# Attention, soft mixture of experts and a gated block in one kernel: one VectorE pass per weight tile instead of two, and a new order of the side work

## The chip, the cores and the metric

One core of a Trainium2 chip runs the whole program. The metric is the device time of one execution in microseconds (us); lower is better. The core has five engines that run their own instruction streams in order and wait for one another through semaphores: TensorE (PE, matrix products; PEld is its loading of weights), VectorE (DVE), ScalarE (ACT), GpSimd (POOL) and SyncE (SP, which here issues every DMA).

## The reference

Three stages follow one another, each in float32:

```python
# attention: q, k, v are (4, 8, 1152, 64); two neighbouring queries are averaged, which leaves 576
scores = scale * matmul(q_pool, k.T);  scores -= max(scores, -1)
attn = exp(scores); attn /= sum(attn, -1) + 1e-9;  x = attn @ v        # x as (2304, 512)
# soft mixture of experts: phi (512, 32), 8 experts with w1 (512, 1024) and w2 (1024, 512)
logits = x @ phi;  d = softmax over rows;  c = softmax over columns
slot_out[e] = relu((d.T @ x)[e] @ w1[e]) @ w2[e];  x = c @ slot_out
# gated block: w_gate, w_val (512, 1536), w_out (1536, 512)
xn = x / sqrt(mean(x*x) + 1e-6) * rms_g;  out = (silu(xn @ w_gate) * (xn @ w_val)) @ w_out
```

The weights of the gated block arrive as float64 words in memory and are turned into float32 on the chip; this is the conversion that the change touches.

## The kernel before

**Attention** works on 16 pairs of heads (`p` = 0 to 15). A pair has 9 key tiles of 128 keys (`kt`) and two halves of 288 queries (`h`). For each key tile and half, `qk` (L360) forms the scores in four products (L369: high and low parts of q and k, and one that subtracts the row's maximum), ScalarE takes the exponential into a tile `e` (L371), and `add_e` (L376) has GpSimd add `e` to a running sum `acc` (L385). `av` (L387) multiplies `e` with v (L391). It is not called for each key tile but after every third one, for three tiles together: these runs of 24 matrix instructions are called *visits* here, and the three key tiles ahead of a visit a *stage*. A pair is thus stage A, visit 1, stage B, visit 2, stage C, visit 3.

The maxima of pair `p+1` are made during pair `p`: 14 items, each a product into PSUM (L318, the last two L325) and a maximum over it by VectorE (L320, L326). `MAX` says how many of the first 12 follow each key tile: before, 2, 2, 1 in stage A, 2, 2, 1 in stage B and 2, 0, 0 in stage C. The last two are `max_tail`.

Scores, maxima and all small products of the side work share one ring of three PSUM buffers of two banks each (tag `u`): the product that takes a buffer waits until the engine that read the one three places earlier is done. The visits write to two other banks (tag `av`).

**Side work** of other pairs is put between the steps of a key tile by the table `AT`: the number ahead of the point is the key tile, the fraction the place within it. Before, a key tile has seven steps (`q0 m q1 m e0 e1 a`, `q` the scores of a half, `m` a maximum, `e` the addition, `a` the visit if one is due), so nothing can be placed inside a visit. For the pair behind (`l = p-1`): `take_x` copies the result out, `sums` and `recips` form the denominators (L410, L419), `x_turn` and `x_divide` transpose and scale (L434, L443), `x_logits`, `x_share` and `logit_add` make the logits (L450, L459, L469 and L470). For the pairs ahead: `load_q`, `load_k`, `load_v` issue DMAs, `sum_q` adds query pairs on GpSimd (L283), `high_q`, `round_k`, `block_q` round on ScalarE (L288, L279, L294), `low_q` and `low_k` take the rest on VectorE (L298, L304), `max_red`, `max_row` and `send_row` bring the maxima into rows (L331, L336, L338, L344). In every fourth pair (`p` = 5, 9, 13) `d_turn`, `d_exp`, `d_back`, `slot_part` and `slot_turn` serve the softmax over rows, and in the pair after it `c_soft` that over columns.

**The conversion.** 36 tiles of 128 x 512 words are loaded (`load_64`), and each takes two instructions on ScalarE (`abs_64`, L658 and L660) and two on VectorE (`turn_64`): L662 shifts the word and fills in the low bits, L663 then brings in the sign. Tiles that are done and aren't kept go back to memory (`spill`, L600), and return in the last stage. `load` (L616) fetches expert weights into whatever buffers are free; buffers come from pools with the tags W, A, B and C, and `KEEP` says how many B buffers the prefetch leaves alone.

Pairs 0 and 15 run half by half (`HALVED`, `STEP_0`), with tables of their own (`AT_0`, `AT_15`).

**After attention** the experts' weights stream through products with 32 columns, and then the gated block runs, bound by its matrix products. The change leaves both as they are, but for the buffers that the prefetch of weights may use.

Of the kernel before, what the change touches and what calls it, by code (L numbers as in the profile page):

```python
# [14 lines left out]
ALU = mybir.AluOpType  # L15
# [15 lines left out]
STEP = "q0 m q1 m e0 e1 a".split()  # L31
STEP_0 = "q m m e a".split()
VISIT = 3
MAX = [2, 2, 1, 2, 2, 1, 2, 0, 0]
AT = dict(
    low_k=[2.8, 2.96],
    low_q=5.84,
    load_v=7.3,
    max_tail=5.79,
    max_red=7.5,  # L40
    max_row=8.78,
    send_row=8.79,
    load_q=4.3,
    load_k=5.73,
    sum_q=6.05,
    high_q=6.8,
    block_q=7.0,
    round_k=[7.8, 8.3],
    take_x=0.5,
    sums=2.79,  # L50
    recips=2.95,
    x_turn=[5.8, 8.8],
    x_divide=[5.81, 8.81],
    x_logits=5.82,
    x_share=5.95,
    logit_add=6.0,
    drop_x=8.82,
    d_turn=0.5,
    d_exp=1.5,
    d_back=2.8,  # L60
    d_copy=2.95,
    slot_part=5.785,
    slot_copy=5.95,
    slot_turn=8.8,
    c_soft=[2.83, 4.5, 5.85],
    load_64=[0.86, 1.65, 4.0],
    abs_64=[2.82, 5.83, 7.4],
    turn_64=[6.2, 6.7, 7.2, 7.7, 8.2, 8.6],
# [14 lines left out]
    send_row=8.79,  # L83
    sum_q=5.91,
# [10 lines left out]
    logit_add=5.22,  # L95
    take_x_a=5.49,
# [23 lines left out]
N_B = 18  # L120
N_C = 42
# [3 lines left out]
KEEP = [7, 6, 12, 6]  # L125
# [14 lines left out]
def attention_softmoe_gated_kernel(ctx: ExitStack, tc: tile.TileContext, kT, qT, vv, ip, cst, w1, w2, wg, wv, wo, rg, out):  # L140
# [235 lines left out]
    def add_e(p, kt, h):  # L376
        e = ets[p, kt, h]
        if kt == 0:
            first[p, h] = e
            return  # L380
        if kt == 1:
            acc[p, h] = B([128, 2, HQ], F32, "acc")
        a = first[p, h] if kt == 1 else acc[p, h]
        eng = dv if p in HALVED and kt % 2 == 0 else gp
        eng.tensor_tensor(out=acc[p, h], in0=a, in1=e, op=ALU.add)  # L385
# [17 lines left out]
    def sums(p, hs=(0, 1)):  # L403

        n = len(hs)
        o = bank([64 * n, HQ], "sums")
        for s in (1, 0):
            for i, h in reversed(list(enumerate(hs))):
                g = 32 * (n * s + i)
                pe.matmul(o[g:g + 32, :], lhsT=ones, rhs=acc[p, h][:, s], start=True, stop=True)  # L410
        rel("B", n)
        srow[p] = B([64 * n, HQ], F32, "srow")
        ac.copy(srow[p], o)
# [235 lines left out]
    def abs_64(n):  # L649

        spill()
        for _ in range(min(n, len(fresh))):
# [5 lines left out]
            ac.activation(w32[key][0], hi.bitcast(F32), AF.Abs, scale=2.0 ** -112)  # L658
            top = raw.bitcast(U16).rearrange("p (n t) -> p n t", t=4)[:, :, 1]
            ac.activation(lo.bitcast(I32), top, AF.Copy, scale=2.0 ** -13, bias=-4095.5 / 8192)  # L660
            turning.extend([
                lambda y=y, lo=lo: dv.scalar_tensor_tensor(out=y, in0=y, scalar=3, in1=lo, op0=ALU.logical_shift_left, op1=ALU.bitwise_or),  # L662
                lambda y=y, hi=hi, key=key: (dv.scalar_tensor_tensor(  # L663
                    out=y, in0=hi, scalar=0x80000000, in1=y, op0=ALU.bitwise_and, op1=ALU.bitwise_or), rel("A"),
                    done.append(key) if key in out_of_chip else None),
            ])
# [7 lines left out]
    def side(p):  # L674
# [11 lines left out]
        if n < NP:  # L686
            at("low_k", lambda i: low_k(n, slice(576 * i, 576 * i + 576)))
            at("low_q", lambda i: low_q(n))
            at("load_v", lambda i: load_v(n))
            if p:  # L690
                at("max_tail", lambda i: (max_item(n, 12), max_item(n, 13)))
            at("max_red", lambda i: max_red(n))
            at("max_row", lambda i: max_row(n))
            at("send_row", lambda i: send_row(n))
# [7 lines left out]
        if l >= 0:  # L702
# [8 lines left out]
            at("logit_add", lambda i: logit_add(l))  # L711
# [15 lines left out]
        if p < NP - 1:  # L727
            at("abs_64", lambda i: abs_64(1))
            at("turn_64", lambda i: turn_64(1))
# [19 lines left out]
    with tc.manual_schedule():  # L749
# [61 lines left out]
        for p in range(NP):  # L811
# [3 lines left out]
            for u, (kt, h) in enumerate(steps):  # L815
# [3 lines left out]
                for i, step in enumerate(order):  # L819
# [11 lines left out]
                    elif kt % VISIT == VISIT - 1:  # L831
                        for k in range(kt - VISIT + 1, kt + 1):
# [415 lines left out]
```

## Time and profile before

| | |
|---|---|
| median of 3 runs | 841.74 us (840.76 to 842.36) |
| the profiled execution | 840.79 us, of which the span from first to last instruction is 839.0 us |
| busy PE / DVE / POOL / ACT | 754.5 / 536.6 / 501.8 / 444.5 us |
| mean granted TensorE clock | 0.963 |
| pairs 1 to 14 of attention | 49.62 to 548.09 us of the span |

Matrix products are pipelined and their ends are modelled, so the busy time of PE is no measure of how full it is; the idle times just before an instruction and what ended them are the better guide. In views of stretches, the columns are the stretch, its length, busy us of each engine with the number of instructions in brackets, the granted clock, the mean busy share of the 16 DMA engines, and GB/s. In lists by line a row gives line, engine, operation, output from inputs, count, then busy us and the mean ns of one, and the idle time ahead of them with what ended it.

### The profile page before, as it was taken

Reading aid. Unit: us, or ns where it says so; the run is one execution under the profiler, and the core shown is the slowest. Engines: PE = TensorE matmul, PEld = TensorE weight load, DVE = VectorE, ACT = ScalarE, POOL = GpSimd, SP = SyncE. Lnnn points to the kernel's source line nnn. Section 1 sums busy time; section 2 is a strip of 40 time slices with the busy share of each in tenths; the row PEclk is TensorE's granted clock in tenths of the full one; section 3 lists DMA queues with packets and bytes.
Section 4 is the critical chain, followed back from the end, with each engine's and each line's share of the span. In section 5 each row is a group of like instructions: output and inputs, shape, how many; then the busy total and the mean of one; then the engine's idle time right before and its main releaser. Section 6 shows DMA issues by size and latency. Waiting matters only on the chain.

```text
span 839.0 us, 15594 instructions
## 1 busy us (share of the span) xinstructions
PE 754.5 (90%) x6015; PEld 516.3 (62%) x6015; DVE 536.6 (64%) x715; ACT 444.5 (53%) x995; POOL 501.8 (60%) x372
## 2 busy tenths in 40 slices
PE   5998989988798897889989798997998999999998
PEld 3555656555465565556556555654444788888887
DVE  6858897796788877688598758724304466545430
ACT  2447566565556656565565546454323686545430
POOL 5448878785777867758697666752200675444330
PEclk9999999998999989999899998999899999999999
DMA  4231531706164351533515313243799210000001
GB/s 153 86 133 42 186 132 67 247 31 220 34 217 144 118 211 52 186 100 125 207 42 186 127 72 126 80 151 127 263 365 385 92 39 24 28 26 16 36 25 38
DMA packets 53001, 103.57 MB, mean 123 GB/s; under 512 B 5832, under 2 KB 19648, under 8 KB 52928
## 3 DMA queue, kind: packets, MB, share of 16 engines
q1 hardware_dynamic: 52928, 102.59, 34.7%
q8 instruction: 47, 0.77, 0.4%
q14 instruction: 26, 0.21, 0.1%
HBM read 89.39 MB, written 13.11 MB: 122 GB/s over the span
## 4 chain that ended last, share of the span: by engine, by line
PE 69%; DVE 14%; ACT 8%; issue 4%; DMA 4%; POOL 0%; SPq 0%; ACTq 0%; DVEq 0%; POOLq 0%
PE yo L1151 18%; PE av L391 16%; PE sc L369 15%; ACT e L371 5%; DVE mx L320 5%; PE mxp L318 4%; DMA w<-in_w_dram 3%; PE gv L1103 3%; DVE w L662 3%; PE xl L450 2%; DVE mx L326 2%; DVE w L663 1%; PE sums L410 1%; PE mxp L325 1%; PE pp L528 1%
## 5 line engine op out<-in xcount | busy, mean ns | idle before, releaser
L385 POOL TENSOR_TENSOR acc<-acc,e 128x576 f32<-128x576 f32 x208 | 329.0, 1613 | 89.9 <-ACT e L371 80.0
L371 ACT ACTIVATE e<-sc 128x576 f32<-128x576 f32 x288 | 184.1, 651 | 216.8 <-PE sc L369 211.8
L320 DVE TENSOR_REDUCE mx<-mxp 128x2 f32<-128x768 f32 x192 | 182.3, 956 | 54.5 <-PE mxp L318 47.9
L391 PE MATMUL av<-e,vt 128*64 128x288 f32 x1152 | 163.5, 434 | 0.3 <-ACT e L371 0.3
L369 PE MATMUL sc<-qh,kh 64*128 64x288 f32 x576 | 109.6, 376 | 22.9 <-DVE mx L320 16.2
L391 PEld LDWEIGHTS av<-e,vt 128*64 128x64 f32 x1152 | 82.4, 145 | 65.9 <-issue 21.5
L369 PEld LDWEIGHTS sc<-qh,kh 64*128 64x128 f32 x576 | 55.5, 188 | 82.3 <-DVE mx L320 53.7
L1151 PE MATMUL yo<-woh,hA 128*128 128x512 f32 (+1 forms) x312 | 98.9, 384 | 0.0
L385 POOL TENSOR_TENSOR acc<-e 128x576 f32<-128x576 f32 x32 | 44.9, 1416 | 80.6 <-ACT e L371 80.5
L369 PE MATMUL sc<-mr,pick 64*128 64x288 f32 x576 | 87.7, 297 | 1.0 <-DMA mr<-mrow 1.0
L369 PE MATMUL sc<-ql,kh 64*128 64x288 f32 x576 | 87.1, 297 | 0.0
L369 PE MATMUL sc<-qh,kl 64*128 64x288 f32 x576 | 87.0, 297 | 0.0
L318 PE MATMUL mxp<-kh,qh 64*128 64x384 f32 x384 | 75.6, 391 | 11.3 <-ACT kh L774 5.7
L1108 DVE SCALAR_TENSOR_TENSOR th<-th,gv 128x384 f32<-128x384 f32 x72 | 39.9, 554 | 62.6 <-ACT th L1105 62.1
L1134 POOL TENSOR_TENSOR hA<-hu,hA 128x384 fp32r<-128x384 f32 x48 | 48.9, 1018 | 42.8 <-ACT hA L1133 38.4
L662 DVE SCALAR_TENSOR_TENSOR w<-w,raw 128x512 uint32<-128x512 uint32 x36 | 64.6, 1795 | 0.0
L1151 PEld LDWEIGHTS yo<-woh,hA 128*128 128x128 f32 x312 | 57.6, 188 | 10.2 <-issue 0.7
L1105 ACT ACTIVATE th<-gv 128x384 f32<-128x384 f32 x72 | 35.3, 490 | 42.7 <-PE gv L1103 40.2
L1151 PE MATMUL yo<-wol,hA 128*128 128x512 f32 (+1 forms) x151 | 57.8, 383 | 0.0
L369 PEld LDWEIGHTS sc<-mr,pick 64*128 64x128 f32 x576 | 56.5, 190 | 1.6 <-DMA mr<-mrow 1.4
L369 PEld LDWEIGHTS sc<-qh,kl 64*128 64x128 f32 x576 | 56.6, 191 | 0.0
L369 PEld LDWEIGHTS sc<-ql,kh 64*128 64x128 f32 x576 | 56.2, 190 | 0.0
(178 smaller groups left out, 1118.1 us busy)
## 6 DMA issues: line engine op xcount, KB each, us to landing
w<-in_w_dram SPq DMA_DIRECT2D x88, 256.0 KB
w<-in_w_dram SPq DMA_DIRECT2D x20, 512.0 KB
vt<-in_vv_dram SPq DMA_DIRECT2D x16, 576.0 KB
qraw<-in_qT_dram SPq DMA_DIRECT2D x15, 576.0 KB
kraw<-in_kT_dram SPq DMA_DIRECT2D x15, 576.0 KB
away<-w SPq DMA_DIRECT2D x32, 256.0 KB
w<-away SPq DMA_DIRECT2D x32, 256.0 KB
raw<-in_wg_dram SPq DMA_DIRECT2D x12, 512.0 KB
```

The lines of the kernel that those rows point to most:

```text
L318: pe.matmul(o[:, s, 0:KC], lhsT=qh[p][r, 128 * t:128 * t + 128], rhs=kh[p][r, KC * c:KC * c + KC], start=True, stop=True)
L320: dv.reduce_max(out=to, in_=o[:, :, 0:KC], axis=AX.X)
L369: pe.matmul(o[:, s, 0:HQ], lhsT=w[r, wk], rhs=q[r, c], start=(i == 0), stop=(i == 3))
L371: ac.activation(ets[p, kt, h], o[:, :, 0:HQ], AF.Exp, scale=0.0625)
L385: eng.tensor_tensor(out=acc[p, h], in0=a, in1=e, op=ALU.add)
L391: pe.matmul(avt[p, h][64 * s:64 * s + 64, 0:HQ], lhsT=vt[p][:, kt, 64 * s:64 * s + 64], rhs=ets[p, kt, h][:, s], start=(kt == 0), stop=(kt ...
L662: lambda y=y, lo=lo: dv.scalar_tensor_tensor(out=y, in0=y, scalar=3, in1=lo, op0=ALU.logical_shift_left, op1=ALU.bitwise_or),
L1103: pe.matmul(o[i], lhsT=sg[n][:, 256 * i + 128 * c:256 * i + 128 * c + 128], rhs=cT[g], start=True, stop=True)
L1105: ac.activation(t, o[0], AF.Tanh, scale=0.5)
L1108: dv.scalar_tensor_tensor(out=t, in0=t, scalar=1.0, in1=o[0], op0=ALU.add, op1=ALU.mult)
L1134: gp.tensor_tensor(out=b, in0=u, in1=f(a), op=ALU.subtract)
L1151: pe.matmul(o, lhsT=x, rhs=w[:, c], start=(ft == 0 and i == 0), stop=(ft == NF - 1 and i == 2))
```

## The change

One VectorE pass per converted tile goes: ScalarE's first instruction becomes `Prelu` with a slope of -2^32 for negative numbers in place of `Abs`, which sets the bit that the shift then moves into the place of the sign. `spill` is called from places of its own. The running sum of `e` becomes two: one over key tiles 0 to 4, one over 5 to 8, and `sums` adds both in PSUM. All 12 maxima come in the first six key tiles. A step `b` is added: `a` now does two key tiles of a visit and `b` the third, so that side work can be placed between them; most places in `AT` are new. B buffers go from 18 to 20, C buffers from 42 to 40, and `KEEP` changes.

```diff
-STEP = "q0 m q1 m e0 e1 a".split()
-STEP_0 = "q m m e a".split()
+STEP = "q0 m q1 m e0 e1 a b".split()
+STEP_0 = "q m m e a b".split()
 VISIT = 3
-MAX = [2, 2, 1, 2, 2, 1, 2, 0, 0]
+PART = 5
+MAX = [2, 2, 2, 2, 2, 2, 0, 0, 0]
 AT = dict(
-    low_k=[2.8, 2.96],
-    low_q=5.84,
+    load_q=0.3,
+    load_k=0.31,
+    sum_q=1.5,
+    high_q=4.6,
+    round_k=[3.6, 5.3],
+    block_q=6.6,
+    low_k=[6.1, 6.3],
+    low_q=6.0,
     load_v=7.3,
-    max_tail=5.79,
-    max_red=7.5,
-    max_row=8.78,
-    send_row=8.79,
-    load_q=4.3,
-    load_k=5.73,
-    sum_q=6.05,
-    high_q=6.8,
-    block_q=7.0,
-    round_k=[7.8, 8.3],
+    max_tail=[2.87, 2.88],
+    max_red=5.9,
+    max_row=7.0,
+    send_row=7.3,
     take_x=0.5,
-    sums=2.79,
-    recips=2.95,
-    x_turn=[5.8, 8.8],
-    x_divide=[5.81, 8.81],
-    x_logits=5.82,
-    x_share=5.95,
-    logit_add=6.0,
-    drop_x=8.82,
-    d_turn=0.5,
-    d_exp=1.5,
-    d_back=2.8,
-    d_copy=2.95,
-    slot_part=5.785,
+    sums=1.9,
+    recips=2.86,
+    x_turn=[5.87, 8.85],
+    x_divide=[5.88, 8.86],
+    x_logits=8.87,
+    drop_x=8.88,
+    x_share=8.95,
+    logit_add=0.3,
+    d_turn=1.91,
+    d_exp=2.1,
+    d_back=2.85,
+    d_copy=2.855,
+    slot_part=5.86,
     slot_copy=5.95,
-    slot_turn=8.8,
-    c_soft=[2.83, 4.5, 5.85],
-    load_64=[0.86, 1.65, 4.0],
-    abs_64=[2.82, 5.83, 7.4],
-    turn_64=[6.2, 6.7, 7.2, 7.7, 8.2, 8.6],
+    slot_turn=8.86,
+    c_soft=[6.35, 7.4, 8.4],
+    load_64=[0.2, 3.0, 8.3],
+    spill=[1.4, 4.4],
+    abs_64=[2.72, 2.73, 5.73],
+    turn_64=[5.72, 7.2, 8.1],
...
-N_B = 18
-N_C = 42
+N_B = 20
+N_C = 40
...
-KEEP = [7, 6, 12, 6]
+KEEP = [10, 6, 12, 12]
...
     def add_e(p, kt, h):
-        e = ets[p, kt, h]
-        if kt == 0:
-            first[p, h] = e
+
+        j = int(kt >= PART)
+        n, e = kt - PART * j, ets[p, kt, h]
+        if n == 0:
+            first[p, h, j] = e
             return
-        if kt == 1:
-            acc[p, h] = B([128, 2, HQ], F32, "acc")
-        a = first[p, h] if kt == 1 else acc[p, h]
+        if n == 1:
+            acc[p, h, j] = B([128, 2, HQ], F32, "acc")
         eng = dv if p in HALVED and kt % 2 == 0 else gp
-        eng.tensor_tensor(out=acc[p, h], in0=a, in1=e, op=ALU.add)
+        eng.tensor_tensor(out=acc[p, h, j], in0=first[p, h, j] if n == 1 else acc[p, h, j], in1=e, op=ALU.add)
...
-        for s in (1, 0):
-            for i, h in reversed(list(enumerate(hs))):
-                g = 32 * (n * s + i)
-                pe.matmul(o[g:g + 32, :], lhsT=ones, rhs=acc[p, h][:, s], start=True, stop=True)
-        rel("B", n)
+        for j in range(2):
+            for s in (1, 0):
+                for i, h in reversed(list(enumerate(hs))):
+                    g = 32 * (n * s + i)
+                    pe.matmul(o[g:g + 32, :], lhsT=ones, rhs=acc[p, h, j][:, s], start=(j == 0), stop=(j == 1))
+        rel("B", 2 * n)
...
-            ac.activation(w32[key][0], hi.bitcast(F32), AF.Abs, scale=2.0 ** -112)
+            ac.activation(w32[key][0], hi.bitcast(F32), AF.Prelu, scale=2.0 ** -112, alpha=-2.0 ** 32)
...
-            turning.extend([
-                lambda y=y, lo=lo: dv.scalar_tensor_tensor(out=y, in0=y, scalar=3, in1=lo, op0=ALU.logical_shift_left, op1=ALU.bitwise_or),
-                lambda y=y, hi=hi, key=key: (dv.scalar_tensor_tensor(
-                    out=y, in0=hi, scalar=0x80000000, in1=y, op0=ALU.bitwise_and, op1=ALU.bitwise_or), rel("A"),
-                    done.append(key) if key in out_of_chip else None),
-            ])
+            turning.append(lambda y=y, lo=lo, key=key: (
+                dv.scalar_tensor_tensor(out=y, in0=y, scalar=3, in1=lo, op0=ALU.logical_shift_left, op1=ALU.bitwise_or),
+                rel("A"), done.append(key) if key in out_of_chip else None))
...
-                at("max_tail", lambda i: (max_item(n, 12), max_item(n, 13)))
+                at("max_tail", lambda i: max_item(n, 12 + i))
...
-            at("logit_add", lambda i: logit_add(l))
+            if p == NP - 1:
+                at("logit_last", lambda i: logit_add(l - 1))
+                at("logit_add", lambda i: logit_add(l))
+            elif l > 0:
+                at("logit_add", lambda i: logit_add(l - 1))
...
                     elif kt % VISIT == VISIT - 1:
-                        for k in range(kt - VISIT + 1, kt + 1):
+                        for k in (kt - 2, kt - 1) if step == "a" else (kt,):
```

## Rows read from the trace of the kernel before

**Rows 1.** The chain that ended last: shares of the span, by engine and by line.
```profile
PE 69%; DVE 14%; ACT 8%; issue 4%; DMA 4%; POOL 0%; SPq 0%; ACTq 0%; DVEq 0%; POOLq 0%
PE yo L1151 18%; PE av L391 16%; PE sc L369 15%; ACT e L371 5%; DVE mx L320 5%; PE mxp L318 4%; DMA w<-in_w_dram 3%; PE gv L1103 3%; DVE w L662 3%; PE xl L450 2%; DVE mx L326 2%; DVE w L663 1%; PE sums L410 1%; PE mxp L325 1%; PE pp L528 1%
```

**Rows 2.** Stretches of pair 8: A, visit 1, B, C, and the pair's sum.
```profile
299.18:305.55 6.37, 6.17 (x66) 4.24 (x67) 5.17 (x6) 4.30 (x8) 2.84 (x3) 1.00 0.91 302
305.55:308.68 3.13, 3.13 (x29) 1.70 (x26) 0.57 (x1) 1.75 (x4) 3.13 (x2) 1.00 1.05 418
308.68:317.76 9.08, 8.49 (x81) 6.22 (x80) 7.88 (x11) 5.30 (x13) 7.07 (x7) 1.00 0.17 69
...
320.89:328.90 8.01, 5.07 (x56) 3.98 (x56) 7.45 (x8) 6.18 (x12) 6.55 (x5) 1.00 0.09 33
...
sum 32.85, PE 29.11 PEld 19.55 DVE 25.14 ACT 19.99 POOL 25.86; mean PE 4.85 PEld 3.26 DVE 4.19 ACT 3.33 POOL 4.31
```

**Rows 3.** The same view of pair 14: stage C and the pair's sum.
```profile
539.86:544.96 5.10, 4.97 (x57) 3.98 (x57) 2.63 (x5) 3.56 (x7) 3.48 (x3) 1.00 0.21 80
sum 29.93, PE 29.02 PEld 19.54 DVE 20.71 ACT 15.35 POOL 21.56; mean PE 4.84 PEld 3.26 DVE 3.45 ACT 2.56 POOL 3.59
```

**Rows 4.** Waits in stage C of pair 8: total us, times, longest us.
```profile
PEld mxt L336 <- ACT kh L279: 1.8, 1, 1.8
PEld sc L369 <- DVE mx L320: 1.7, 2, 1.5
...
PE sc L369 <- DVE mx L320: 1.2, 1, 1.2
```

**Rows 5.** VectorE in pair 8 in order of time: start us, us.
```profile
300.12 5.04 DVE L320 TENSOR_REDUCE mx<-mxp 128x2 f32<-128x768 f32 x5 [2.29 <-PE mxp L318]
...
322.70 1.78 DVE L662 SCALAR_TENSOR_TENSOR w<-w,raw 128x512 uint32<-128x512 uint32 x1
```

**Rows 6.** Lines over the whole span.
```profile
L385 POOL TENSOR_TENSOR acc<-acc,e 128x576 f32<-128x576 f32 x208 | 329.0, 1613 | 89.9 <-ACT e L371 80.0 <-DVE acc L385 9.9
L371 ACT ACTIVATE e<-sc 128x576 f32<-128x576 f32 x288 | 184.1, 651 | 216.8 <-PE sc L369 211.8 <-POOL acc L385 1.1 <-PE mxp L318 0.7
...
L663 DVE SCALAR_TENSOR_TENSOR w<-raw,w 128x512 uint32<-128x512 uint32 x36 | 54.3, 1507 | 0.3
...
L470 DVE TENSOR_TENSOR lg<-lg,ls 96x192 f32<-96x192 f32 (+1 forms) x13 | 12.0, 925 | 0.4
...
L469 DVE TENSOR_TENSOR lg<-lg,ls 96x192 f32<-96x192 f32 (+1 forms) x13 | 9.8, 754 | 0.4
```

**Rows 7.** Line L470 alone: shortest, median and longest in ns.
```profile
L470 DVE TENSOR_TENSOR lg<-lg,ls x13: 253/1440/1447, 105.3 to 583.9; 96x192 f32<-96x192 f32 x11, 96x96 f32<-96x96 f32 x2
```

**Rows 8.** Small products of pair 8 on TensorE: start us, us.
```profile
308.61 0.53 PE L419 MATMUL sumt<-cs,srow 128*96 128x128 f32 x3
...
314.93 0.79 PE L325 MATMUL mxp<-kh,tb 128*128 128x384 f32 x3
...
315.81 0.53 PE L434 MATMUL xo<-cs,xu 128*96 128x128 f32 x3
...
316.59 1.23 PE L450 MATMUL xl<-ipt,xu 128*96 128x64 f32 x12 [0.26 <-DVE mx L326]
```

**Rows 9.** Stretches: pairs 1 to 4, 6 to 8, 10 to 12, summed.
```profile
sum 343.57, PE 303.95 PEld 201.54 DVE 278.97 ACT 206.97 POOL 266.96; mean PE 101.32 PEld 67.18 DVE 92.99 ACT 68.99 POOL 88.99
```

**Rows 10.** Stretches: pair 9, and pairs 5, 9 and 13 summed.
```profile
332.03:372.46 40.43, 34.20 (x304) 22.08 (x303) 28.84 (x34) 22.53 (x51) 27.32 (x18) 0.96 0.37 129
...
sum 124.97, PE 106.59 PEld 69.33 DVE 85.58 ACT 67.64 POOL 80.90; mean PE 35.53 PEld 23.11 DVE 28.53 ACT 22.55 POOL 26.97
```

**Rows 11.** Stretches: visit 3 of pair 7, and most of the experts' part.
```profile
293.64:299.18 5.54, 5.54 (x27) 2.64 (x26) 4.16 (x3) 1.32 (x6) 3.64 (x3) 0.56 0.32 105
...
599.50:650.00 50.50, 47.47 (x517) 21.62 (x516) 11.63 (x31) 14.53 (x35) 3.52 (x9) 1.00 1.03 373
```

**Rows 12.** The DMA queue's own waits over the span: total us, times, longest.
```profile
SPq L600 <- DVE w L663: 210.5, 14, 22.1
```

**Rows 13.** ScalarE's load of a function table, the only one in the span.
```profile
L768 ACT ACT_TABLE_LOAD x1 | 1.3, 1283 | 0.7 <-PEq L1237 0.7
```

More of the change, by code (lines that the diff above doesn't have):

```diff
@@ L83 @@
     send_row=8.79,
+    load_q=4.3,
+    load_k=5.73,
     sum_q=5.91,
@@ L95 @@
     logit_add=5.22,
+    logit_last=0.3,
     take_x_a=5.49,
@@ L649, in abs_64 @@
     def abs_64(n):
-        spill()
         for _ in range(min(n, len(fresh))):
@@ L727, in side @@
         if p < NP - 1:
+            at("spill", lambda i: spill())
             at("abs_64", lambda i: abs_64(1))
```

## The prediction, as it was recorded before the change was run

> **What bounds the kernel now.** I read the chain that ended last first. TensorE is 69% of it, but VectorE 14%, and within that the two conversion passes have 3% and 1% [rows 1]: some 34 us of the span end on a conversion, which is no part of attention at all. Next I cut a pair without disturbance, pair 8, into its stages and visits. All three visits take 3.13 us (one is shown) and the stages 6.37, 9.08 and 8.01 [rows 2]. In stage C, TensorE has 5.07 us of work in 8.01. Its waits name the reasons: two score products stood behind maxima, 1.7 and 1.2 us, and the transposition of the maxima waited 1.8 us for ScalarE's rounding of k [rows 4]. VectorE's order in time says why the maxima were late: a conversion pass of 1.78 us starts at 322.70, amid the maxima of key tile 6 [rows 5]. Pair 14 is the control that the kernel carries with it: it has the same products but nothing to convert and no pair to round for. Its stage C is 5.10 us and the pair 29.93, against 8.01 and 32.85 [rows 2, 3]. So conversion and rounding cost 2.9 us a pair there, and nowhere else.
>
> In stage A the limit is another. Five maxima run back to back from 300.12, 5.04 us in all, 1.007 each [rows 5]; ScalarE has 4.30 us and GpSimd 2.84 us of work in 6.37 [rows 2]. VectorE sets the pace wherever maxima come two to a key tile.
>
> The ten plain pairs (1 to 4, 6 to 8, 10 to 12) take 343.57 us, 34.36 each [rows 9], 1.51 above pair 8. Part of that is the clock: visit 3 of pair 7 takes 5.54 us at a granted clock of 0.56 [rows 11], that is, mostly at 1.2 instead of 2.4 GHz, right after a stage C in which TensorE waited.
>
> **The change part by part, for a plain pair.**
>
> *Stage A.* VectorE's first maximum starts 0.94 us into the stage [rows 2, 5], and the fourth ends 4 x 1.007 later, at 4.97; the old stage ends 1.40 after that. In the new order the denominators' product goes ahead of the last key tile, and behind the fourth maximum come one maximum product, the last scores and another: 1.0. But `logit_add` now stands between the first two maxima, where before it lay in the visit's shadow. Its two additions are 0.75 and 0.93 us on average [rows 6], and TensorE waits through them, since each buffer of the ring needs its maximum. 4.97 + 1.68 + 1.0 = 7.65. The bounds come from the same line: 0.25 to 1.45 us an addition [rows 7], so 0.5 to 2.9 for both. I take the mean.
>
> *Visit 1.* 3.13, the transposition of the denominators (0.53) and the tail of the maxima (0.79) [rows 8]: 4.45. Four instructions of ScalarE for two conversions (each about 0.69 us, 2.75 in all) go ahead of the visit and lie beside it; without that cover they would cost 2.75.
>
> *Stage B.* The old stage less all from the tail at 314.93 on (2.83) and less 0.4 for the denominators is 5.85 [rows 2, 8]. A sixth maximum at its end adds its product, 0.2. Three roundings come in, 0.67 us each, on a ScalarE that has 6 x 0.65 us of exponentials [rows 6]: 5.9 in all against 6. I add 0.3; bounds 0 and 1.2 (two of the three exposed). 6.35.
>
> *Visit 2.* 3.13 + 0.53 for a transposition = 3.66. One conversion is hidden beside it on ScalarE. On VectorE a conversion pass, the low parts of q and k and later two more passes follow, some 8 us, in visit 2 and stage C, where no maximum stands behind them any more. What is late next there is ScalarE.
>
> *Stage C.* No maxima, no casts of k. Six exponentials take 3.9 us, the block of q and the row of maxima 0.75 more on ScalarE; TensorE leaves two exponentials before the end. I take 4.2. Bounds: 3.4 (scores alone, no wait), 5.1 (pair 14's).
>
> *Visit 3.* 3.13 + 0.53 + 1.23 for the logits' product [rows 8] = 4.89.
>
> Sum: 7.65 + 4.45 + 6.35 + 3.66 + 4.2 + 4.89 = 31.2. The visits are cut in four places; with 0.1 us a cut, 31.6. That is 1.25 below pair 8. Of the 1.51 by which the mean of plain pairs exceeds pair 8 I keep half, 0.75, since stage C has less waiting but stage A more: 32.35 (bounds 31.6 and 33.1). Pair 1 has no `logit_add`: 30.7. Ten pairs: 9 x 32.35 + 30.7 = 321.9, a gain of 21.7.
>
> *Pairs 5, 9, 13* take 124.97 us together; pair 9 is 7.6 above pair 8 [rows 2, 10]. Their products stay, but three of them go into visits, where no wait on the ring stands ahead of them; I take 6.6 instead of 7.6. 31.6 + 0.75 + 6.6 = 38.95, times 3 = 116.9: a gain of 8.1.
>
> *Pair 14* has nothing to convert or round, so it gains nothing and bears the new `logit_add` and the moved maxima: 31.6 less 0.3 and 0.7 = 30.6, a loss of 0.7.
>
> *The first pass on ScalarE* with another function on the same operands: no row shows it. The nearest are activations of as many elements at about 0.69 us, so I take no difference; a tenth either way would be hidden in the visits. *The partial sums* save two of GpSimd's 16 additions a pair, 2 x 1.61 = 3.2 us [rows 6], off the path: in the 31.6 us of a new pair GpSimd has 14 x 1.61 + 1.5 = 24.1. They add a second set of products of the denominators, under half a microsecond, beside VectorE's maxima in stage A; without that cover, 0.5 a pair. *The buffers*: three tiles of weights fewer (0.26 MB each) may be waiting when attention ends, while the experts' part moves 373 GB/s with the DMA engines full [rows 11]: 0 to 2.1 us. With pair 15's second set of products I add 1.0 for the end.
>
> Together: -21.7 - 8.1 + 0.7 + 1.0 = -28.1. The profiled execution took 840.79, so 812.7; the median of the runs lies 0.95 higher: **813.6 us**.
>
> *A rule against it.* GpSimd's additions and VectorE's `logit_add` meet here: the second addition took anything from 0.25 to 1.45 us [rows 7]. The Trainium skill, "SBUF — State Buffer", section "SBUF: two separate sides", says that VectorE with two SBUF inputs and GpSimd contend for a port pair that is locked for a whole instruction, the other blocking fully. The spread in the row agrees with it. By the rule at its worst both additions in stage A wait, and the sum is rival 1's.
>
> **The rivals.**
>
> *1. The additions in stage A meet GpSimd* (chance 0.22). The median of the second is 1.44 us [rows 7], near the upper bound. For it: a shorter stage C leaves GpSimd further behind at the start of the next pair. Against it: GpSimd has two additions fewer. Price 2.9 - 1.7 = 1.2 in 13 pairs, 15.6: 829 us.
>
> *2. More than the sum* (0.14). Nothing of the low clock stays (-0.75) and stage C reaches 3.4 (-0.8): 1.55 x 13 = 20, so 793 us. Against it: pair 14's stage C without conversions was 5.1.
>
> *3. Slower: the sum of queries holds GpSimd* (0.05). `sum_q` moves from key tile 6 to key tile 1, and its DMA is issued only at 0.3 of the same pair. SyncE issues in order, and its spills waited 210.5 us in 14 places for VectorE, 15 each [rows 12]. If such a wait stands ahead of q, GpSimd's additions queue behind `sum_q`, then the denominators and buffers of `e` behind them. GpSimd has 31.6 - 24.1 = 7.5 us to give; from there each microsecond is one of the pair. At 11 us late: 3.5 x 13 = 45 more, 859 us. Against it: in the new order the spills stand behind the loads, and what they wait for was done in the pair before.
>
> *4. Slower or even: the slope is in another function table* (0.03). One table load of 1.28 us in the span serves all functions now [rows 13]. Two more around each group of conversions make ScalarE 5.3 us in visit 1 (of 4.45) and 5.3 in visit 2 (of 3.66): 2.5 late a pair. It decides from 2.2 a pair on, the gain spread over 13 pairs. 2.5 x 12 = 30: 844 us. Against it: exponential, absolute value, hyperbolic tangent and square already share one. The Trainium skill, "ScalarE: Activation LUTs", section "Table sets: the hidden batching unit", says that cheap functions such as relu and abs are in every set; it does not name the slope function, and no run here shows it.
>
> *5. No gain* (0.03): the pass was covered and ScalarE holds stage C as before: 841. Pair 14 speaks against it.
>
> **How the numbers follow.** Forecast 0.53, with a range of its own from 801 to 826; the rivals as given. Faster (by over 0.2%, about what a measurement of this kernel can tell): 0.53 + 0.22 + 0.14 = 0.89; same 0.03; slower 0.05 + 0.03 = 0.08. The unknown terms are +-15 (additions), +-10 (clock) and +-11 (stage C); as independent ones they make some 21 us either way. That gives 792 to 837; a little over one in ten is above it, less than one in ten below.
>
> **What would show it.** Stage C of a pair at 4 to 4.5 us with no wait of scores on maxima; stage A longer, 7 to 8.5, with the additions between maxima; L663's passes gone, and the single pass per tile at 1.3 to 1.9 us; visits 4.5, 3.7 and 4.9; one table load; SyncE's spill waits far below 210 us. I am wrong if plain pairs stay above 34 us, if GpSimd waits on the DMA of q, or if stage A grows past 9 us.

## The result and the profile after

The changed kernel takes **785.32 us** (median of 3 runs, 784.09 to 786.75) against 841.74: a ratio of 0.9332, 95% interval 0.9303 to 0.9361. The gain is 56 us where 28 were forecast, and the time lies below the range of 792 to 837. Run again beside the experiments it took 785.78. The kernel before, with nothing changed, took anything from 830.5 us at a mean granted clock of 0.979 to 843.2 at 0.957 there.

The chain that ended last, by engine and by line, of the changed kernel (the view of [rows 1]; the lines of the file have moved: scores are L374, the visits L397, the one conversion pass L669):

```profile
PE 83%; DVE 8%; DMA 3%; ACT 3%; issue 2%; SPq 0%; ACTq 0%; DVEq 0%
PE av L397 20%; PE sc L374 19%; PE yo L1160 19%; DVE mx L325 6%; PE mxp L323 4%; PE gv L1112 3%; PE sums L417 3%; PE xl L457 2%; ACT e L376 2%; PE xo L441 2%; PE hin L929 2%; PE mxp L330 2%; DMA w<-away 1%; PE so L952 1%; DMA w<-in_w_dram 1%
```

TensorE's share rises from 69 to 83%, and no conversion is among the lines any more. Pair 8 in its six stretches (A, visit 1, B, visit 2, C, visit 3; the columns of [rows 2]), and then pairs 1 to 14 together:

```profile
269.83:277.29 7.46, 6.78 (x77) 4.74 (x77) 5.17 (x7) 4.56 (x9) 3.69 (x3) 1.00 1.03 341
277.29:281.38 4.09, 4.09 (x32) 2.18 (x30) 2.29 (x5) 2.63 (x5) 4.09 (x4) 1.00 1.06 394
281.38:287.81 6.43, 6.21 (x61) 4.46 (x62) 5.36 (x6) 4.38 (x8) 4.67 (x5) 1.00 0.05 16
287.81:291.56 3.75, 3.75 (x31) 1.91 (x29) 3.64 (x7) 3.38 (x10) 1.11 (x1) 1.00 0.28 63
291.56:295.57 4.01, 3.99 (x50) 3.38 (x51) 1.22 (x3) 3.37 (x10) 2.45 (x2) 1.00 0.23 91
295.57:300.30 4.73, 4.73 (x43) 2.99 (x41) 0.55 (x1) 2.15 (x8) 4.73 (x5) 1.00 0.43 118
sum 30.47, PE 29.55 PEld 19.64 DVE 18.22 ACT 20.47 POOL 20.74; mean PE 4.92 PEld 3.27 DVE 3.04 ACT 3.41 POOL 3.46
```
```profile
51.19:492.22 441.03, 425.16 (x4020) 279.47 (x4020) 267.82 (x389) 284.09 (x634) 288.60 (x209) 1.00 0.42 144
```

Stage C is half of what it was, with TensorE at work for 3.99 of 4.01 us; stage A is longer by 1.1 us, B shorter by 2.6, and the three visits together longer by 3.2 for the products put into them. The granted clock over all these pairs is 1.00 in this execution; in the one profiled beside the experiments a single stage, A of pair 11, lost it (10.04 us at 0.83 instead of 7.46), and the pairs took 443.52. Pairs 1 to 14 took 498.47 us before, 343.57 and 124.97 of it in the thirteen that convert [rows 9, 10] and 29.93 in pair 14 [rows 3], and take 441.03 now: 57.4 less. The rest of the program gives back 0.7 of that.

VectorE and GpSimd by line (the view of [rows 6]):

```profile
L391 POOL TENSOR_TENSOR acc<-acc,e 128x576 f32<-128x576 f32 x148 | 205.7, 1418 | 75.2 <-ACT e L376 64.5 <-DVE acc L391 10.6
...
L669 DVE SCALAR_TENSOR_TENSOR w<-w,raw 128x512 uint32<-128x512 uint32 x36 | 23.9, 685 | 0.0
...
L476 DVE TENSOR_TENSOR lg<-lg,ls 96x192 f32<-96x192 f32 (+1 forms) x13 | 5.5, 426 | 0.1
L477 DVE TENSOR_TENSOR lg<-lg,ls 96x192 f32<-96x192 f32 (+1 forms) x13 | 5.5, 425 | 0.4
```

This I had not foreseen. Not only is the second pass gone (54.3 us [rows 6]): the pass that stays takes 685 ns, where the one in pair 8 took 1.78 us [rows 5], the additions of the logits 0.43 each for 0.75 and 0.93, and GpSimd's additions 1.418 for 1.613. VectorE and GpSimd hinder each other less; the experiment with one sum below shows where.

### The profile page after: what moved, and what is told of

Same layout as the page of the kernel before. It is cut to its first block, busy times and chain, and to the rows that moved or that the text cites. A ratio compares the mean times of both kernels' runs of the same rounds, so it can differ in the third digit from the quotient of the medians.

```text
span 782.3 us, 15697 instructions
## 1 busy us (share of the span) xinstructions
PE 742.3 (95%) x6143; PEld 506.4 (65%) x6143; DVE 420.6 (54%) x679; ACT 439.0 (56%) x995; POOL 414.9 (53%) x340
## 4 chain that ended last, share of the span: by engine, by line
PE 83%; DVE 8%; DMA 3%; ACT 3%; issue 2%; SPq 0%; ACTq 0%; DVEq 0%
PE av L397 20%; PE sc L374 19%; PE yo L1160 19%; DVE mx L325 6%; PE mxp L323 4%; PE gv L1112 3%; PE sums L417 3%; PE xl L457 2%; ACT e L376 2%; PE xo L441 2%; PE hin L929 2%; PE mxp L330 2%; DMA w<-away 1%; PE so L952 1%; DMA w<-in_w_dram 1%
## 5 line engine op out<-in xcount | busy, mean ns | idle before, releaser
L376 ACT ACTIVATE e<-sc 128x576 f32<-128x576 f32 x288 | 181.1, 648 | 139.2 <-PE sc L374 133.9
L391 POOL TENSOR_TENSOR acc<-acc,e 128x576 f32<-128x576 f32 x148 | 205.7, 1418 | 75.2 <-ACT e L376 64.5
L397 PE MATMUL av<-e,vt 128*64 128x288 f32 x1152 | 162.8, 418 | 0.2 <-ACT e L376 0.2
L391 POOL TENSOR_TENSOR acc<-e 128x576 f32<-128x576 f32 x60 | 84.3, 1425 | 82.2 <-ACT e L376 82.2
L374 PE MATMUL sc<-qh,kh 64*128 64x288 f32 x576 | 107.3, 368 | 10.3 <-DVE mx L325 5.2
L397 PEld LDWEIGHTS av<-e,vt 128*64 128x64 f32 x1152 | 74.4, 137 | 56.0 <-issue 16.6
L374 PEld LDWEIGHTS sc<-qh,kh 64*128 64x128 f32 x576 | 54.3, 184 | 67.5 <-DVE mx L325 31.6
L374 PE MATMUL sc<-mr,pick 64*128 64x288 f32 x576 | 86.0, 293 | 1.0 <-DMA mr<-mrow 1.0
L374 PE MATMUL sc<-qh,kl 64*128 64x288 f32 x576 | 85.7, 293 | 0.0
L374 PE MATMUL sc<-ql,kh 64*128 64x288 f32 x576 | 85.6, 293 | 0.0
L450 ACT ACTIVATE xt<-xo,rr 96x64 f32<-96x64 f32 x186 | 41.0, 310 | 36.7 <-PE xo L441 36.6
L374 PEld LDWEIGHTS sc<-mr,pick 64*128 64x128 f32 x576 | 55.0, 186 | 1.4 <-DMA mr<-mrow 1.4
L374 PEld LDWEIGHTS sc<-qh,kl 64*128 64x128 f32 x576 | 55.2, 187 | 0.0
L374 PEld LDWEIGHTS sc<-ql,kh 64*128 64x128 f32 x576 | 54.9, 186 | 0.0
```

The lines of the kernel that those rows point to most:

```text
L374: pe.matmul(o[:, s, 0:HQ], lhsT=w[r, wk], rhs=q[r, c], start=(i == 0), stop=(i == 3))
L376: ac.activation(ets[p, kt, h], o[:, :, 0:HQ], AF.Exp, scale=0.0625)
L391: eng.tensor_tensor(out=acc[p, h, j], in0=first[p, h, j] if n == 1 else acc[p, h, j], in1=e, op=ALU.add)
L397: pe.matmul(avt[p, h][64 * s:64 * s + 64, 0:HQ], lhsT=vt[p][:, kt, 64 * s:64 * s + 64], rhs=ets[p, kt, h][:, s], start=(kt == 0), stop=(kt ...
L450: ac.activation(xts[j // 3][:, j % 3, p % 4, c], o[:, i, c], AF.Copy, scale=r[:, j, s:s + 1])
```

## The experiments

Theory S, formed after the result: the new order takes VectorE's passes away from the maxima, and with no waits in stage C the clock stays up. Rivals: the second pass itself was the cost (P); the place of the maxima alone (M). All comparisons below are of medians; beside these experiments the median of the kernel before was 838.0 to 841.5. In the edits, code is cut short.

**The conversion alone, in the old order.**

```diff
 # the kernel before
-ac.activation(w32[key][0], hi.bitcast(F32), AF.Abs, scale=2.0 ** -112)
+ac.activation(w32[key][0], hi.bitcast(F32), AF.Prelu, scale=2.0 ** -112, alpha=-2.0 ** 32)
-turning.extend([first pass, second pass])
+turning.append(first pass)
```

> The kernel before with only the conversion changed (slope on ScalarE, one VectorE pass a tile), all places as before. Theory S (the new order takes VectorE's passes away from the maxima, and the clock stays up because TensorE no longer waits in stage C): in the old order a pass still stands between the two maxima of key tile 6 and the roundings of k still stand in stage C, so 1 us or so a pair: 822 to 838 us. Rival P (the second pass itself was the cost): most of the 56 us come from here, 785 to 805 us.

816.22 us, ratio 0.9737 (0.9708 to 0.9767): 22 us. More than S gave, far less than P. Stage C is 6.5 in pairs 8, 10 and 12 and 7.4 or more in the other pairs that convert; low clock remains in five stretches of pairs 1 to 14, against ten before. Why the pass alone is worth so much, stage C of pair 8 in the kernel before shows (start, us; idle time in brackets): TensorE's last wait there is for L331, which reduces the maxima to a row, and that stands behind two passes on VectorE.

```profile
325.27 1.02 DVE L663 SCALAR_TENSOR_TENSOR w<-raw,w 128x512 uint32<-128x512 uint32 x1
326.21 1.89 DVE L662 SCALAR_TENSOR_TENSOR w<-w,raw 128x512 uint32<-128x512 uint32 x1
328.03 0.17 DVE L331 TENSOR_REDUCE mxw<-mx 128x9 f32<-128x27 f32 x1
328.34 0.30 PE L336 MATMUL mxt<-cs,mxw 128*128 128x128 f32 x1 [1.61 <-DVE mxw L331]
```

With the single pass one of the two is gone, and this wait with it; the wait for a maximum, 1.2 us, remains. The third visits are 4.5 us above 3.13 each in sum, for 11.3 before.

**Both passes back, in the new order.**

```diff
 # the changed kernel
-AF.Prelu, scale=2.0 ** -112, alpha=-2.0 ** 32
+AF.Abs, scale=2.0 ** -112
-turning.append(first pass)
+turning.append((first pass, second pass))
```

> The changed kernel with the absolute value and both VectorE passes back, in the new places. Theory S: stage C stays at 4.0 to 4.5 us, as no maximum stands behind the passes; VectorE has some 4 us more in visit 2 to visit 3, which hold about as much room, so the next stage A may start up to 1 us late: 786 to 800 us. Rival P: 815 us or more, with the low clock back in visit 3.

788.7 us, ratio 0.9418 (0.9378 to 0.9459): only 3 us above the changed kernel. Stage C is 4.0 in pairs 1 to 12, as S says; stage A bears the rest (7.9 in pairs 3, 4 and 8, 9.75 in pair 11). P falls: what the pass costs depends on who stands behind it.

**More work for TensorE in stage C, to part the clock from the waits** (products that nothing reads).

```diff
 # the kernel before, in qk, for kt >= 6 and 0 < p < 15 (e3: twice, behind the exponential; e3b: once, ahead of the scores)
+for s in range(2):
+    r = slice(64 * s, 64 * s + 64)
+    pe.matmul(o[:, s, HQ:512], lhsT=kh[p][r, k], rhs=qh[p][r, 0:512 - HQ], start=True, stop=True)
```

> The kernel before with four products more behind the scores of each half in stage C of pairs 1 to 14 (into columns of the buffer that nobody reads), so that TensorE works while it waits for maxima and roundings; no dependency on VectorE changes. Theory S with the clock as a term of its own: stage C grows by a few tenths at most, the low clock goes, visit 3 is 3.1 us in every pair: 826 to 836 us, which sizes the clock's share at 6 to 15 us. Rival (the low clock has another cause than TensorE's waits in stage C): clock as before, 842 us or more.

922.89 us, ratio 1.0982 (1.0927 to 1.1038). The experiment missed its aim: the products shared the exponential's buffer and waited for it, which this line of TensorE shows (columns as in [rows 6]; the idle time is the last figure):

```profile
L376 PE MATMUL sc<-qh,kh 64*128 64x224 f32 x336 | 48.9, 376 | 68.5 <-ACT e L371 68.5
```

Stage C grew to 11.8 to 15.4 us, and visit 3 to 3.7 to 5.3 in all pairs but one: more waiting there brought more of the low clock, not less. Put ahead of the scores:

> The kernel before with two products more ahead of the scores of each half in stage C of pairs 1 to 14, into columns that nobody reads: they stand ahead of the exponential, so they wait for nothing that the scores do not wait for, unlike the four of the earlier try, which stood behind the exponential. Theory S with the clock as a term of its own: TensorE's work in stage C rises by about 1.5 us, the stage by under 0.6, the low clock in visit 3 goes or is rarer: 826 to 840 us. Rival (the low clock has another cause): visit 3 as before, 842 us or more.

838.11 us, ratio 0.9988 (0.9946 to 1.0029): no difference. Low clock falls in six stretches of pairs 1 to 14 instead of ten, but this execution (834.8 us) lies near the low end of the filler kernel's 833.6 to 842.2, and the filler itself costs 0.1 to 0.5 us a stage. The clock's share is not settled by this.

**The maxima.** First back to the old places in the changed kernel, then moved alone in the kernel before, then with the single pass:

```diff
 # e5, the changed kernel; e5b has max_red=7.5, max_row=8.78, send_row=8.79 as before
-MAX = [2, 2, 2, 2, 2, 2, 0, 0, 0]
+MAX = [2, 2, 1, 2, 2, 1, 2, 0, 0]
-    max_red=5.9,
+    max_red=6.9,
 # e10, the kernel before; e11 has the conversion of e1 besides
-MAX = [2, 2, 1, 2, 2, 1, 2, 0, 0]
+MAX = [2, 2, 2, 2, 2, 2, 0, 0, 0]
```

> The changed kernel with the maxima of the first nine key tiles as before (2, 2, 1, 2, 2, 1, 2), so that two of them stand in stage C behind a conversion pass and the low parts of q and k; the reduction over them is placed after them. Theory S: stage C grows from 4.0 to 6 us or more, stages A and B fall by 0.3 to 0.5 each: 792 to 812 us. Rival (where the maxima stand is of no account once one pass is gone): 780 to 786 us.

854.89 us, ratio 1.0158 (1.0055 to 1.0262). Too much, and for a reason of its own: the row of maxima at 7.0 then waits for VectorE's whole backlog.

> As e5 (the changed kernel with the old places of the maxima in stage C), but with their reduction, their row and its DMA at the old places 7.5, 8.78 and 8.79, so that no transposition waits at 7.0 behind VectorE's backlog, which cost 4.3 us in a stage C of e5. Theory M: the two maxima alone still stand behind the low parts and a pass: stage C 5.5 to 7.5 us, 800 to 825 us. Rival (e5 was slow for the transposition alone): 783 to 790 us.

811.62 us, ratio 0.968 (0.9587 to 0.9773): 26 us above the changed kernel. Stage C is 5.8 us in ten pairs, at the full clock; only in three others (6, 10 and 14) does the clock fall. VectorE in pair 8's visit 2 and stage C (start, us) shows the two maxima behind the side work:

```profile
299.16 1.79 DVE L669 SCALAR_TENSOR_TENSOR w<-w,raw 128x512 uint32<-128x512 uint32 x1
300.87 0.74 DVE L303 TENSOR_TENSOR ql<-qs,qh 128x576 fp32r<-128x576 f32 x1
301.54 0.75 DVE L309 TENSOR_TENSOR kl<-kraw,kh 128x576 fp32r<-128x576 f32 x1
303.70 0.96 DVE L325 TENSOR_REDUCE mx<-mxp 128x2 f32<-128x768 f32 x1 [1.41 <-PE mxp L323]
304.57 1.77 DVE L309 TENSOR_TENSOR kl<-kraw,kh 128x576 fp32r<-128x576 f32 x1
306.27 0.95 DVE L325 TENSOR_REDUCE mx<-mxp 128x2 f32<-128x768 f32 x1
```

> The kernel before with only the maxima moved: two after each of the first six key tiles, none in stage C; both conversion passes and all places as before. After the earlier runs, theory M (most of the gain is that nothing that TensorE waits for stands behind VectorE's side work in stage C): stage C falls from 8.0 to 6 to 6.8 us (ScalarE's roundings remain), A and B grow by 0.3 to 0.6 each, the low clock becomes rarer: 805 to 825 us. Rival (the maxima and the removed pass are two halves of one cost, and moving either alone gives the 22 us of the pass alone at best): 818 us or more.

842.75 us, ratio 1.0058 (1.0018 to 1.0098): no gain at all, and theory M in its plain form falls. Stage C of pair 8 and the visit behind it (columns as in [rows 2]):

```profile
321.93:328.03 6.10, 4.40 (x53) 3.63 (x53) 3.58 (x5) 5.17 (x11) 4.47 (x3) 1.00 0.12 44
328.03:332.80 4.77, 4.77 (x27) 2.34 (x26) 0.00 (x0) 1.91 (x9) 4.22 (x4) 0.65 0.04 6
```

Stage C gained 1.9 us, A and B lost 0.4 and 0.5, and visit 3 lost 1.6 at a granted clock of 0.65. Visit 3 lost clock in every pair from 2 to 13: their third visits are 17.8 us above 3.13 each in sum. VectorE has 3.58 us of work in that stage C; ScalarE has 5.17, and TensorE's waits there are for it (total us, times, longest):

```profile
PE sc L369 <- ACT e L371: 1.0, 1, 1.0
...
PE xo L434 <- ACT e L371: 0.7, 1, 0.7
```

In pair 7, ScalarE in order of time:

```profile
289.51 0.68 ACT L288 CAST qh<-qs 128x576 fp32r<-128x576 f32 x1
...
291.95 0.67 ACT L658 ACTIVATE w<-raw 128x512 f32<-128x512 f32 x1
292.53 0.65 ACT L660 ACTIVATE raw<-raw 128x512 int32<-128x512 uint16 x1
293.08 0.65 ACT L279 CAST kh<-kraw 128x576 fp32r<-128x576 f32 x1
...
294.71 0.66 ACT L279 CAST kh<-kraw 128x576 fp32r<-128x576 f32 x1
```

Roundings, and a conversion besides, stand between the exponentials.

> The kernel before with the maxima moved and the single conversion pass, all places as before. Theory M: the pass adds little once no maximum stands behind it: within 6 us of the maxima alone, 800 to 820 us. Rival: the two gains add up, the maxima's and the 22 us of the pass: 790 us or less.

844.3 us, ratio 1.0061 (1.002 to 1.0101), and both expectations missed: the same stage C of 6.1 (7.2 to 7.5 in plain pairs with a conversion in it) and the same low clock. The single pass, worth 22 us alone, is worth nothing here: what it takes out of stage C is a wait on VectorE, and with the maxima moved ScalarE comes last.

**ScalarE's roundings.** Back in stage C in the changed kernel, and out of it, together with the maxima, in the kernel before (where the loads and the sum of queries had to move with them):

```diff
 # e8, the changed kernel
-high_q=4.6, block_q=6.6, round_k=[3.6, 5.3]
+high_q=6.8, block_q=7.0, round_k=[7.8, 8.3]
 # e13, e10 with these besides (AT_0 keeps load_q=4.3, load_k=5.73)
-max_red=7.5, load_q=4.3, load_k=5.73, sum_q=6.05, high_q=6.8, block_q=7.0, round_k=[7.8, 8.3]
+max_red=5.9, load_q=0.3, load_k=0.31, sum_q=1.5, high_q=4.6, block_q=6.6, round_k=[3.6, 5.3]
```

> The changed kernel with the roundings alone back in stage C (queries at 6.8, block at 7.0, k at 7.8 and 8.3); the maxima stay out of it, one pass, two sums, cut visits. Theory C (two engines held stage C, VectorE through the maxima and ScalarE through the roundings, and only a stage C with neither keeps TensorE dense enough for the full clock ahead of visit 3): stage C about 6.1 us as with the maxima alone, visit 3 above 4.74 by 1 us or more at a lower granted clock, stage B 0.1 to 0.4 shorter: 805 to 830 us. Rival V (VectorE's side work is what counts, ScalarE has room): 784 to 792 us, clock as in the changed kernel.

794.7 us, ratio 0.9507 (0.944 to 0.9574): 9 us above the changed kernel run beside it. In the profiled execution, the fastest of the four at 789.81 us, stage C is 4.58 and no clock is lost in pairs 1 to 14; it lies 5 to 6 us above the changed kernel's profiled ones. The other three (794 to 798 us) had a lower mean granted clock, 0.983 to 0.989 against 0.994, and where they lost it isn't shown. Theory C (VectorE and ScalarE both held stage C) overstated the roundings, V (only VectorE did) understated them.

> The kernel before with the maxima out of stage C (their reduction at 5.9) and the loads, the sum of queries and the roundings at the changed kernel's places; two passes, one running sum, whole visits and all other places as before. Theory C: these two moves together are most of the 56 us, though the maxima alone gave none: stage C 4.0 to 4.8, visit 3 3.13, no low clock in most pairs: 785 to 805 us. Rival V: the roundings add nothing to the maxima alone: 835 us or more.

816.32 us, ratio 0.9762 (0.9695 to 0.9828). Between the two again: 26 us below the maxima alone. Stage C is 4.67 in pairs 8, 10 and 12, with visit 3 at 3.13; in the plain pairs with a conversion at 7.4 it is 5.9 to 6.3, and four of those seven have a visit 3 of 4.4 to 4.8. Those stages hold the two ScalarE instructions of a conversion besides, some 1.3 us; I take these for the third thing that had to leave stage C, which no run tests by itself.

**One running sum in the changed kernel.**

```diff
-PART = 5
+PART = 9
-        for j in range(2):
+        for j in range(1):
...
```

> The changed kernel with one running sum again: 16 additions a pair on GpSimd and 8 instructions for the denominators' product in place of 16. If the second set of products stands on the path in stage A, as the timeline with the moved logits makes me think (1.18 us between two maxima), that stage falls by 0.5: 777 to 782 us. Rival (GpSimd then finishes too late for the denominators at 1.9): stage A grows by 1 us or more, 795 us or more.

796.51 us, ratio 0.9506 (0.9442 to 0.957): 11 us above. My rival had the time right, and GpSimd is late as it said; but it is not the denominators that TensorE waits for. VectorE in pair 8 of this kernel, then of the changed one (start, us):

```profile
290.15 1.88 DVE L303 TENSOR_TENSOR ql<-qs,qh 128x576 fp32r<-128x576 f32 x1
291.95 2.64 DVE L309 TENSOR_TENSOR kl<-kraw,kh 128x576 fp32r<-128x576 f32 x2
294.51 3.72 DVE L669 SCALAR_TENSOR_TENSOR w<-w,raw 128x512 uint32<-128x512 uint32 x2
```
```profile
289.49 0.74 DVE L303 TENSOR_TENSOR ql<-qs,qh 128x576 fp32r<-128x576 f32 x1
290.16 1.41 DVE L309 TENSOR_TENSOR kl<-kraw,kh 128x576 fp32r<-128x576 f32 x2
291.49 1.28 DVE L669 SCALAR_TENSOR_TENSOR w<-w,raw 128x512 uint32<-128x512 uint32 x2
```

And GpSimd beside it, in the same order:

```profile
285.41 7.89 POOL L391 TENSOR_TENSOR acc<-acc,e 128x576 f32<-128x576 f32 x5
293.84 8.41 POOL L391 TENSOR_TENSOR acc<-acc,e 128x576 f32<-128x576 f32 x5 [0.54 <-ACT e L376]
```
```profile
284.76 4.16 POOL L391 TENSOR_TENSOR acc<-acc,e 128x576 f32<-128x576 f32 x3
293.12 2.80 POOL L391 TENSOR_TENSOR acc<-e 128x576 f32<-128x576 f32 x2 [4.20 <-ACT e L376]
```

With two sums key tile 5 begins a sum and adds nothing, so GpSimd stands idle for 4.20 us in visit 2 and the start of stage C, and that is where VectorE's side work lies: 3.4 us for these five instructions, 8.2 with one sum. But nothing waits for them there: stage C is 4.00 with one sum too, and pair 8 only 0.17 us longer. The loss is in stage A of pairs 7, 9, 11 and 13 (8.50, 11.10, 10.78 and 12.49 us for 7.45, 9.71, 7.46 and 9.73) and in visit 1 of pair 13 (6.59 for 4.49, at a granted clock of 0.66). GpSimd, two additions further behind, is still adding or sums queries when the logits' additions come. Pair 11 of the kernel with one sum (start, us):

```profile
360.26 10.34 POOL L391 TENSOR_TENSOR acc<-acc,e 128x576 f32<-128x576 f32 x6 [0.54 <-ACT e L376]
370.55 1.51 POOL L288 TENSOR_TENSOR qs<-qraw 128x576 f32<-128x576 f32 x1
...
369.19 1.62 DVE L476 TENSOR_TENSOR lg<-lg,ls 96x192 f32<-96x192 f32 x1
370.84 1.44 DVE L477 TENSOR_TENSOR lg<-lg,ls 96x192 f32<-96x192 f32 x1
...
373.20 0.61 PE L374 MATMUL sc<-qh,kh 64*128 64x288 f32 x2 [2.90 <-DVE mx L325]
```

TensorE waits 2.90 us for the maximum behind them, and the granted clock of the stage is 0.84.

**The visits whole.**

```diff
-for k in (kt - 2, kt - 1) if step == "a" else (kt,):
+for k in range(kt - 2, kt + 1) if step == "a" else ():
```

> The changed kernel with each visit in one piece: step a does all three key tiles, b nothing, so the products that stood inside now stand behind the visit, in the same order. Theory S: the same products, but what VectorE and ScalarE make of them is no longer covered and the next stage starts with the ring in use: 0.3 to 1.0 us a pair, 789 to 799 us. Rival (the inside is of no use; TensorE has the same work): 784 to 787 us.

787.91 us, ratio 0.9407 (0.935 to 0.9464): 2 us above. The products inside the visits are worth 0.15 us in most plain pairs, 0.5 to 0.6 in two; pair 11 lost 2.7 to a late addition of the logits (1.61 us) and a stage A of 11.70 at a granted clock of 0.85, which the changed kernel itself shows in its second profile.

**A version that beats the change.** The logits' additions at 2.5, in the shadow of visit 1, except in pairs 5, 9 and 13; then the denominators earlier too:

```diff
-                at("logit_add", lambda i: logit_add(l - 1))
+                at("logit_add" if p % 4 == 1 else "logit_mid", lambda i: logit_add(l - 1))
+    logit_mid=2.5,
 # e9 besides
-    sums=1.9,
+    sums=1.3,
```

> The changed kernel with the addition of the logits moved from between the first two maxima of stage A into the shadow of visit 1 (place 2.5), except in pairs 5, 9 and 13, where the softmax needs it. Theory S: stage A is paced by VectorE, so it falls from 7.46 to about 6.7 us in ten pairs: 775 to 780 us. Rival (stage A is paced by TensorE or ScalarE): 785 us as before.

780.78 us, ratio 0.9317 (0.9285 to 0.9348). Stage A falls to 7.11 in the pairs that had 7.46, not to 6.7.

> The changed kernel with the logits' addition at 2.5 outside pairs 5, 9, 13 (as e4) and the denominators' product at 1.3 in place of 1.9, between maxima that VectorE sets the pace for. If the 1.18 us of that product stands on the path at 1.9, stage A falls from 7.1 to 6.0 to 6.6: 769 to 778 us. Rival (GpSimd's last additions are not done by 1.3): 785 us or more.

786.44 us, ratio 0.9393 (0.9318 to 0.9468): a miss; stage A is 7.24 and pairs 5, 9 and 13 lose 0.7 and more. The rival's reason isn't it in pair 3, where GpSimd's additions end 2.6 us before the product starts; the maxima behind it come later instead, with VectorE idle for 1.36 us. The changed kernel and the version with the logits moved, on one chip, six runs each:

> The changed kernel as it is, beside the others on one chip: 0.933 of the kernel before by every theory (781 to 787 us).

785.78 us, ratio 0.9406 (0.9357 to 0.9455).

> The kernel of e4 (logits' addition at 2.5) beside the changed kernel on one chip. Its trace shows stage A at 7.11 instead of 7.46 in seven pairs, so 2 to 3 us less than the changed kernel run beside it, if that is all; the rival says no difference beyond 0.5 us.

782.21 us, ratio 0.9364 (0.931 to 0.9418). The ratios' intervals overlap, since the kernel before scatters, but the six runs (780.0 to 783.1) lie all below the changed kernel's six (784.5 to 786.9): 3.6 us.

## Why the prediction was wrong

The direction, the place (stage C) and the main mechanism (VectorE's and ScalarE's side work leaves it) were right; the size was half of what came. Pair 8, term by term:

| | A | visit 1 | B | visit 2 | C | visit 3 | sum | allowances | plain pair |
|---|---|---|---|---|---|---|---|---|---|
| forecast | 7.65 | 4.45 | 6.35 | 3.66 | 4.2 | 4.89 | 31.2 | 0.4 + 0.75 | 32.35 |
| measured | 7.46 | 4.09 | 6.43 | 3.75 | 4.01 | 4.73 | 30.47 | none | 30.47 |

**The step that failed is the allowance.** "Of the 1.51 by which the mean of plain pairs exceeds pair 8 I keep half, 0.75, since stage C has less waiting but stage A more", and 0.1 us for each cut of a visit. Nothing of either remained: 1.15 us in 13 pairs, 15 of the 28 us by which the forecast fell short. The granted clock of pairs 1 to 14 is 1.00; before, their third visits alone were 11.3 us above 3.13 each. TensorE is busy 5.07 of 8.01 us in stage C of pair 8 before [rows 2], 4.40 of 6.10 with the maxima moved alone, with the low clock in every visit 3 but those of pairs 1 and 14, and 3.99 of 4.01 in the changed kernel. No visit 3 behind a stage C of that last kind lost any clock. But waiting in stage C does not always cost it: pair 8 before kept 1.00 in its visit 3, with 2.9 us of waiting, where pair 8 with the maxima moved lost it after 1.7. What decides between them is not shown. Nor did I hold the clock up by itself (e3, e3b), so its share is not measured apart. The spread of the kernel before allows an estimate: 830.5 us at 0.979 and 843.2 at 0.957 make 5.8 us for each 0.01, so the step from its usual 0.963 to the changed kernel's 0.991 would be some 16 of the 56 us, if the line holds beyond 0.979.

**The stage terms** were 0.73 too high in sum, 9.5 us in 13 pairs, the first visit (0.36), A and C (0.2 each) above all. Stage A was near for the wrong reasons. The additions cost 0.35 of the 1.68 that I put, as stage A of 7.11 without them shows, and as pairs 2, 6, 10 and 14 do, where one addition comes instead of two (7.1; the prediction gave them two). The 0.25 that I took from [rows 7] for the lower bound is that of the two additions of half size. The stage without them is 7.1, not 5.97: the denominators' product, now 1.18 us, stands on the path there, where I had it hidden beside the maxima.

**One reading was wrong**, though no term hangs on it: that the transposition of the maxima waited 1.8 us for ScalarE's rounding of k [rows 4]. That row is of its weight load; the product itself waited 1.61 us for VectorE's row of maxima, as the rows in the experiment with the conversion alone show. And the 1.2 us of the score product lie within its weight load's 1.7, so one maximum was waited for at length, not two. VectorE ended both long waits of that stage C; ScalarE came last only once VectorE's part was gone (6.10 us with the maxima moved). So the pass was worth 22 us alone.

**Pairs 5, 9 and 13** take 35.34, 35.33 and 35.62 instead of 38.95. Their own products cost 4.9 above a plain pair, not 6.6: another 5 us. **Pair 1** (31.62 for 30.7) and **pair 14** (29.87 for 30.6) are within 1 us. The end gave 0.7 of the 1.0 put.

**"Off the path" for the partial sums was wrong.** I counted GpSimd's saved time and saw none of it on the path; undone alone, they cost 11 us, in stage A. What counts is when GpSimd is idle. Because VectorE met it less, the sign "the single pass at 1.3 to 1.9 us" was wrong too (0.69; 1.16 with one sum).

**The rivals.** The first, the additions against GpSimd, did not come in the first profile (0.43 us each on average), but its mechanism is there with one sum, and once in the second profile of the changed kernel: in pair 11 the second addition lasts 1.46 us beside `sum_q` on GpSimd, TensorE waits 1.66 us for the next maximum, and the clock falls. The second had the sign and the clock right, and stage C's size wrong (4.0, not 3.4). The third shows in the trace, harmless: `sum_q` waits for the DMA of q in seven places, as this row of who waited for whom has it,

```profile
POOL qs L288 <- DMA qraw<-in_qT_dram: 21.9, 7, 3.8
```

which GpSimd's slack takes. The fourth did not come: the changed kernel loads one table.

```profile
L777 ACT ACT_TABLE_LOAD x1 | 1.3, 1283 | 0.7 <-PEq L1246 0.7
```

**Where the 56 us are.** Undone one at a time from the changed kernel: maxima 26, partial sums 11, roundings 9, the second pass 3, the visits' inside 2, some 51 in all. Done on the kernel before: the pass alone 22, the maxima alone none, pass and maxima none, maxima and roundings 22. So the parts don't add, and that the undone ones come near 56 proves no complete account. With the maxima moved and ScalarE still holding stage C, the time won went into the clock of visit 3. The places of the spills and the numbers of buffers, which the change also sets, were not tried by themselves.

## What to carry to other kernels

Clear a stage of every engine's side work, not of the one that waits longest: list what each engine does there, and expect little from one move if a second engine then holds the stage: moving the maxima alone gave nothing, though undoing them cost 26 us. Price an instruction by what runs beside it in its new place: the same pass took 1.8 us next to GpSimd and 0.69 without. And where low clock follows a waiting stage, and the change ends the waiting altogether, count all of it as part of that stage's price, not half; where it only shortens the waiting, the clock may take the gain back.

## What the runs showed of the hardware

VectorE's instructions with two operands in SBUF took from 1.9 to 2.9 times as long while GpSimd added: the low part of q 0.74 us against 1.88, the low parts of k 0.70 against 1.32 each, a conversion pass 0.64 against 1.86, in the rows of the experiment with one sum. The Trainium skill, "SBUF — State Buffer", section "SBUF: two separate sides", names a port pair that the two engines share and lock for a whole instruction; the traces agree. The maxima, which read PSUM, took 0.96 us in all kernels.

TensorE at 1.2 instead of 2.4 GHz came right after stages in which it had waited, and it cost visit 3 between 0.8 and 2.5 us a time in the kernel before and with the maxima moved: a stage shortened by 1.9 us returned 1.6 of it so (maxima alone, pair 8). Not every such stage was followed by it: in pair 8 of the kernel before the granted clock stayed at 1.00.

A slope of -2^32 on ScalarE costs what the absolute value did (0.690 us against 0.688 for 128x512); no second table load came with it.
